# One attention tile further ahead, the hidden-layer halves moved to the end of each step, and a wider PSUM ring for the last products

## The chip, the cores and the metric

One core of a Trainium2 chip runs the whole program. The metric is the device time of one execution in microseconds; below, a number without a unit is in microseconds. TensorE is called PE, VectorE DVE, ScalarE ACT, GpSimd POOL, and SyncE, which issues the transfers, SP.

## The reference

Three layers follow each other on 1536 tokens (2 batches of 768) of width 512.

```python
# attention: 8 heads of 64; local window |i-j| < 16, plus 24 block summaries
k_sum = k.reshape(B, H, nb, 32, D).max(axis=3);  v_sum = v.reshape(...).mean(axis=3)
scores = concat(mask_local(scale * q @ k.T), scale * q @ k_sum.T + log(32))
a = softmax(scores);  x = a @ concat(v, v_sum)
# mixture of 8 experts, width 1024: all experts on all tokens, Sinkhorn weights P (8 rounds)
x = sum_e P[:, e] * (relu(x @ w1[e]) @ w2[e])
# last layer, width 2048, with a rational activation
h = x @ w_in;  y = (poly3(h; a) / (1 + |b0||h| + |b1|h^2 + 1e-6)) @ w_out
```

## The kernel before, in words

All large products are done in three passes of a split into a high and a low part (`mm3`, lines 184 to 186), so PE carries most of the work. Nothing is reordered by a planner: every engine takes its instructions in the order in which the program writes them, and an instruction that waits holds up all that stand behind it on its engine.

**Attention** works on tiles of 64 tokens (24 of them; `QT`, `NQ`) in a loop of 27 steps `s`. A tile `t` passes through these functions:
- `scores(t)`: 16 matmuls into one PSUM tile `sc` (one buffer), then four mask-and-minimum instructions on DVE (L631) that write the SBUF tile `a` (three buffers).
- `exps(t)`: four exponentials on ACT (L641).
- `norm(t)`: three DVE instructions, add (L651), reciprocal (L652) and multiply (L653). The small results of the first two lie in spare columns of the PSUM tile `xo` for `t` below 11 and in the SBUF tile `sm` after that.
- `trans(t)`: four transposes on PE (L659) into a PSUM tile `tr` (two buffers), copied out by ACT (L661).
- `av(t)`: 16 matmuls (L678) into the PSUM tile `xo`, then the split of the result into `xh` (ACT, L687) and `xl` (DVE, L688).

Step `s` writes, for PE, `scores(s)`, `av(s-3)`, half of its share of the first expert's work, `trans(s-2)`, in steps 3 to 5 three filler matmuls (`spin(3)`), the transposes of coming k or q tiles (`prep_k`, `prep_q`), and the other half of its share. For DVE it writes the masks of `scores(s)`, the `xl` of `av(s-3)`, the post of a hidden tile if one is due (`hl`, L263), and `norm(s-1)`. The share is one or two half products a step from step 7 on (`share`, `main`); a half of the first product (`g1_halves`) has six matmuls of 256 columns, a half of the second (`g2_halves`) six of 512.

The start is special. Tiles 0 to 2 are scored while data still arrives. Step 2 sums the first two blocks of v (`prep_v`). Step 3 does `trans(1)`, `exps(3)`, `norm(2)`, the last block of v, a copy of v's block means on DVE into the value tile `vx[0]` (L568), q's second tile (`prep_q(0, 1)`) and `av(0)`. POOL then copies the means into `vx[1]` and `vx[2]` (`block_values`) at the end of that step. POOL also makes the block keys and the edges of the key windows ready (`blocks_to`, `halos`). At step 15, `gate_parts` (lines 356 to 359) prepares the expert gate with one ACT and three DVE instructions.

**The experts** run afterwards in 60 blocks `block(v, j)`, each with seven products of 384 columns (L1229 to L1231) and, in `g2w`, six groups of six matmuls of 512 columns into PSUM tiles `p_v`, each added to the result by one DVE instruction (L1341). These tiles come from a ring of three (`psm`); from the third half unit on (`v >= VG`) the six groups of a block stand together. In block (1, 1) DVE does the first part of a conversion of the last layer's weights (`cv_join(0)`) ahead of `product(5)`'s hidden tile.

Of the kernel before, what the change touches and what calls it, by code (L numbers as in the profile page):

```python
# [10 lines left out]
F32 = mybir.dt.float32  # L11
# [11 lines left out]
def kernel(  # L23
# [330 lines left out]

    def gate_parts():
        nc.scalar.activation(coef[:, 4:6], coef[:, 4:6], AF.Abs)
        nc.vector.tensor_scalar_mul(coef[:, 0:4], coef[:, 0:4], -1.0)
        nc.vector.tensor_copy(wgs[:, :, 0:NE], wgr)
        nc.vector.tensor_sub(wgs[:, :, 32:32 + NE], wgr, wgs[:, :, 0:NE].bitcast(F32))


    TPIECE = HT // 4
# [3 lines left out]
    with ExitStack() as actx:  # L366
# [163 lines left out]
        def prep_q(b, i):  # L530
            new_q(b, i)
            for par in range(2):
                place(qT[b, i], par, transpose8("q", b, i, par), qscale, (b, i) == (0, 2))
# [13 lines left out]
            nc.gpsimd.tensor_add(s, t[:, :, 0, :], t[:, :, 1, :])  # L547
            nat["vsum", b, i] = s

        def prep_v(b, *parts):  # L550
            if parts[0] == 0:
                vps[b] = psm.tile([P, DM], F32, tag="mm", name=f"vps_{b}")
            ps = vps[b]
            nb = LT // BLK
            for i in parts:
                o = (NB - nb) - nb * i
                if i == NL - 1:
                    t = nat.pop(("v", b, i))
                    rs_ = [t[:, :, y, :] for y in range(2)]
                else:  # L560
                    rs_ = [nat.pop(("vsum", b, i))]
                for n, r in enumerate(rs_):
                    nc.tensor.matmul(
                        ps[SO:SO + NB, :].rearrange("p (h d) -> p h d", h=H), lhsT=wavg[:, o:o + NB], rhs=r,
                        start=(i == 0), stop=n == 1, tile_position=(0, SO),
                    )
            if parts[-1] == NL - 1:
                nc.vector.tensor_copy(vx[0][SO:SO + NB, :], ps[SO:SO + NB, :])  # L568
                vs[b] = vx[0]

        def means_split(i):
            x = nat.pop(("vsum", 1, i)).rearrange("p h d -> p (h d)")
# [32 lines left out]
        def scores(t):  # L605
            b, r = divmod(t, QB)
            qt = qT[b, r // TPL]
            if t == 1:
                ps = [psa.tile([P, NP, P], F32, tag="tr", name=f"sc_{t}_{x}", bufs=2) for x in range(2)]
            else:  # L610
                ps = psa.tile([P, 2, NP, P], F32, tag="sc", name=f"sc_{t}")
                ps = [ps[:, x] for x in range(2)]
            w = kw[:, slot(t)]
            i = 0 if r == 0 else (2 if r == QB - 1 else 1)
            m = masks[i]
            o = r % TPL * QT
            for p in range(NP):
                x = p % 2
                p = x * (NP // 2) + p // 2
                for j in range(2):  # L620
                    h = slice(j * D, (j + 1) * D)
                    y = (j ^ x) * D
                    nc.tensor.matmul(
                        ps[x][y:y + D, p % (NP // 2), 0:CO], lhsT=qt[h, p, o:o + QT], rhs=w[h, p, :],
                        start=True, stop=True, tile_position=(j * D, y),
                    )
            a = apool.tile([P, NP, CO], F32, tag="a", name=f"a_{t}", bufs=3)
            sm = apool.tile([P, 4, NP], F32, tag="sm", name=f"sm_{t}", bufs=3)
            for p in range(NP):
                p = p % 2 * (NP // 2) + p // 2  # L630
                nc.vector.tensor_tensor_reduce(  # L631
                    out=a[:, p, :], in0=ps[p // (NP // 2)][:, p % (NP // 2), 0:CO], in1=m[:, 0, :],
                    scale=-1.0, scalar=3.0e38, op0=ALU.add, op1=ALU.min, accum_out=sm[:, 0, p:p + 1],
                )
            st[t] = (a, sm, a)

        def exps(t):
            a, sm, x = st[t]
            for p in range(NP):
                p = p % 2 * (NP // 2) + p // 2  # L640
                nc.scalar.activation(  # L641
                    a[:, p, :], x[:, p, :], AF.Exp, scale=-1.0, bias=sm[:, 0, p:p + 1], accum_out=sm[:, 1, p:p + 1]
                )

        def norm(t):
            a, sm, _ = st[t]
            e, r = sm[:, 2, :], sm[:, 3, :]
            if t < QB - 1:
                o = st["xo"]
                e, r = o[:, 0, QT:QT + NP], o[:, 1, QT:QT + NP]  # L650
            nc.vector.tensor_scalar_add(e, sm[:, 1, :], 1e-9)  # L651
            nc.vector.reciprocal(r, e)  # L652
            nc.vector.tensor_mul(a, a, r.unsqueeze(2).to_broadcast([P, NP, CO]))  # L653

        def trans(t):
            a = st.pop(t)[0]
            ps = psa.tile([P, NP * P], F32, tag="tr", name=f"at_{t}", bufs=2)
            for p in range(NP):
                nc.tensor.transpose(ps[0:CO, p * P:(p + 1) * P], a[:, p, :], ident)  # L659
            aT = apool.tile([CO, NP * P], F32, tag="aT", name=f"aT_{t}")  # L660
            nc.scalar.copy(aT, ps[0:CO, :])  # L661
            st[t, "aT"] = aT
# [121 lines left out]
        def at(s, f, *args):  # L784
            todo.setdefault(s, []).append(lambda: f(*args))
# [8 lines left out]
        for i in range(NL):  # L794
            if i:
                at(8 + i, edge_after, 1, i)
            at(8 + i, halos, 1, i)
        at(10, blocks_to, 1, 0, TPL)
        at(12, blocks_to, 1, TPL, QB)
        at(3, load_nat, k, "k", 1, 0)  # L800
# [6 lines left out]
        at(15, load_tok, q, "q", 1, 2)  # L807
        at(7, load_nat, v, "v", 1, 0)
        at(8, load_nat, v, "v", 1, 1)
        at(8, load_tok, q, "q", 1, 0)  # L810
        at(9, load_nat, v, "v", 1, 2, 8)
        at(5, dma_w, 0, 2, 0, 6)
        at(7, dma_w, 0, 2, 1)
        for t in range(1, 3):
            at(3, block_values, t)
        order = [(7 + i, "k", 1, i) for i in range(NL)]
# [6 lines left out]
            at(W1[c][1], low_w1, c)  # L823
            at(W2[c], split_w2, c)
        for i in range(NL):
            at(min(8 + i, 9), block_keys, 1, i)
            at(9 + i, sum_v, 1, i)
        for i in range(NL):
            at(10 + i, means_split, i)
# [25 lines left out]
                    mains.append((ready, 0, f, NCH, h))  # L855
        share = dict(zip(range(7, 26), (2, 2, 2, 2, 2, 2, 2, 2, 2, 2, 1, 1, 2, 2, 2, 1, 1, 2, 2)))

        def main(s, end):
            n = share.get(s, 0)
            for _ in range((n + 1) // 2 if end and n < 3 else n // 2 if not end and n < 3 else 1 if end else 2):  # L860
                assert mains[0][0] <= s
                mains.pop(0)[2]()

        for s in range(NQ + AV):
            if s == 2:
                norm(0)
            if s < NQ:
                scores(s)
            if s == 2:
                prep_v(0, 0)  # L870
                prep_v(0, 1)
                norm(1)
                exps(2)
                trans(0)
                by_token_half(0)
                by_token_half(1)
            if s == AV:
                trans(1)
                exps(3)
                norm(2)  # L880
                prep_v(0, 2)
                prep_q(0, 1)
            if s >= AV:
                av(s - AV)
                if s - AV + 3 < NQ:
                    load_vx(s - AV + 3)
                flush()
            main(s, False)
            if AV < s < NQ + AV - 1:
                trans(s - AV + 1)  # L890
            if 2 < s < 6:
                spin(3)
            if AV < s <= NQ:
                norm(s - 1)
            if s < NQ and s not in (2, AV):
                exps(s)
            for f in todo.pop(s, []):
                f()
            main(s, True)
        assert not todo  # L900
        flush()
        assert not mains[0][4]
# [301 lines left out]

    late = []
    held = []

    def step(v):
        tick()

    def block(v, j):
# [9 lines left out]
        def tt(i):  # L1221
            return lambda t: (th[i][:, t, ot:ot + n], tl[i][:, t, ot:ot + n])
# [83 lines left out]
        nc.vector.tensor_add(s3, s3, Y)  # L1306
        hidden(1, 1, s3)
        step(v)
        if first:
            cv_join(0)  # L1310
        product(5, X, tt(2), False)
        hidden(1, 0, X)
        step(v)
        product(6, Y, xs(1, o2), False)
        nc.vector.tensor_add(s2, s2, Y)
# [7 lines left out]
    def g2w(v, j, half, t):  # L1323
        g = (j * HT + half * NW) // P + t
        u = UW + v // 2
        ps = psm.tile([P, 512], F32, tag="mm", name=f"p2_v{v}_{g}")
        o = t * P

        def get(c):
            hh, hl = ht["v", v, j, c, half]  # L1330
            return (hh[:, o:o + P], hl[:, o:o + P]), wt["v", v, c]

        mm3(ps, 2, get)
        a, e = acc[g], u // UPE
        if e == 0:
            nc.vector.tensor_add(a, a, ps)
        else:
            if u == UPE and v % 2 == 0:
                assert not jobs
                acc_scale(g)  # L1340
            nc.vector.scalar_tensor_tensor(  # L1341
                out=a, in0=ps, scalar=Pt[:, g, e:e + 1], in1=a, op0=ALU.mult, op1=ALU.add
            )
        if v == NSUB - 1:
            jobs.append((point[0] + 2, lambda: to_x(g)))
# [107 lines left out]
```

## Time and profile before

| | us |
|---|---|
| median of 3 runs (1358.25 to 1358.62) | 1358.3 |
| the profiled execution | 1359.21 |
| its span, from the first to the last instruction | 1357.5 |

| engine | busy in the span | share |
|---|---|---|
| PE | 1346.4 | 99% |
| DVE | 1056.3 | 78% |
| POOL | 805.3 | 59% |
| ACT | 511.9 | 38% |

Busy time of PE runs to the modelled end of each matmul, and the next one may begin before that end. So a short wait of PE does not show as idle time; it shows as a longer distance between the starts of two matmuls. The attention loop lasts from about 13 to 106 of the span, the expert blocks with the wide ring's candidates (`v >= VG`) from about 206 to 1068.

### The profile page before, as it was taken

Reading aid. Unit: us, or ns where it says so; the run is one execution under the profiler, and the core shown is the slowest. Engines: PE = TensorE matmul, PEld = TensorE weight load, DVE = VectorE, ACT = ScalarE, POOL = GpSimd, SP = SyncE. Lnnn points to the kernel's source line nnn. Section 1 sums busy time; section 2 is a strip of 40 time slices with the busy share of each in tenths; the row PEclk is TensorE's granted clock in tenths of the full one; section 3 lists DMA queues with packets and bytes.
Section 4 is the critical chain, followed back from the end, with each engine's and each line's share of the span. In section 5 each row is a group of like instructions: output and inputs, shape, how many; then the busy total and the mean of one; then the engine's idle time right before and its main releaser. Section 6 shows DMA issues by size and latency. Waiting matters only on the chain.

```text
span 1357.5 us, 20289 instructions
## 1 busy us (share of the span) xinstructions
PE 1346.4 (99%) x7343; PEld 1183.8 (87%) x7343; DVE 1056.3 (78%) x1959; ACT 511.9 (38%) x1134; POOL 805.3 (59%) x982
## 2 busy tenths in 40 slices
PE   8999999999999999999999999999999999999999
PEld 6878998889988899988999988999888888888887
DVE  7875588777777777777777777777777689988885
ACT  6874323322222222222222222222222369866662
POOL 7714647777776777777777776777777013222221
PEclk9999999999999999999999999999999999999999
DMA  9730112222222222222222222222222421213102
GB/s 260 168 84 1 47 35 74 76 83 71 78 68 72 67 68 76 68 80 72 85 75 74 67 72 69 68 76 67 83 70 65 134 74 47 89 37 93 31 16 78
DMA packets 122004, 102.40 MB, mean 75 GB/s; under 512 B 36272, under 2 KB 102960, under 8 KB 121904
## 3 DMA queue, kind: packets, MB, share of 16 engines
q1 hardware_dynamic: 121904, 101.10, 25.8%
q8 instruction: 58, 0.95, 0.3%
q14 instruction: 42, 0.34, 0.1%
HBM read 81.15 MB, written 19.92 MB: 74 GB/s over the span
## 4 chain that ended last, share of the span: by engine, by line
PE 96%; DVE 2%; ACT 1%; DMA 1%; issue 0%; SPq 0%; POOL 0%; DVEq 0%; ACTq 0%
PE p_v L184 12%; PE p_v L185 12%; PE p_v L186 12%; PE p L184 8%; PE p L186 8%; PE p L185 8%; PE X L1229 6%; PE X L1231 6%; PE X L1230 6%; PE Z L1231 3%; PE Z L1230 3%; PE Z L1229 3%; PE Y L1231 2%; PE Y L1230 2%; PE Y L1229 2%; PE xo L678 1%
## 5 line engine op out<-in xcount | busy, mean ns | idle before, releaser
L1341 DVE SCALAR_TENSOR_TENSOR accs<-p_v,Pt,accs 128x512 f32<-128x512 f32 x336 | 244.3, 745 | 89.5 <-PE p_v L186 88.8
L184 PE MATMUL p_v<-w2h_v,hh_v 128*128 128x512 f32 x720 | 283.3, 393 | 0.2
L186 PE MATMUL p_v<-w2h_v,hl_v 128*128 128x512 f32 x720 | 281.7, 391 | 0.0
L185 PE MATMUL p_v<-w2l_v,hh_v 128*128 128x512 f32 x720 | 281.5, 391 | 0.0
L1238 DVE SCALAR_TENSOR_TENSOR hl_v<-s,hh_v 128x384 fp32r<-128x384 f32 x180 | 137.5, 764 | 75.8 <-ACT hh_v L1237 74.6
L234 POOL TENSOR_TENSOR hl<-ta,hh 128x512 fp32r<-128x512 f32 x48 | 62.4, 1301 | 204.6 <-ACT hh L233 152.9
L1249 ACT COPY s<-X 128x384 f32<-128x384 f32 x56 | 27.1, 483 | 410.4 <-PE X L1231 410.4
L1039 POOL TENSOR_SCALAR ce<-ce 128x296 uint32<-128x296 uint32 (+1 forms) x56 | 67.2, 1200 | 180.2 <-DVE ce L1030 180.2
L184 PEld LDWEIGHTS p_v<-w2h_v,hh_v 128*128 128x128 f32 x720 | 135.2, 188 | 31.8 <-issue 6.2
L186 PEld LDWEIGHTS p_v<-w2h_v,hl_v 128*128 128x128 f32 x720 | 135.1, 188 | 28.7
L185 PEld LDWEIGHTS p_v<-w2l_v,hh_v 128*128 128x128 f32 x720 | 135.2, 188 | 25.5
L1237 ACT ACTIVATE hh_v<-s 128x384 fp32r<-128x384 f32 x180 | 94.9, 527 | 126.7 <-DVE s L1272 68.8
L110 POOL TENSOR_TENSOR wS<-S,wS 128x256 fp32r<-128x256 f32 x120 | 100.0, 834 | 14.4 <-ACT wS L107 4.7
L184 PE MATMUL p<-xh,w1h 128*128 128x512 f32 (+2 forms) x272 | 101.3, 373 | 0.0
L186 PE MATMUL p<-xh,w1l 128*128 128x512 f32 (+2 forms) x272 | 99.0, 364 | 0.0
L185 PE MATMUL p<-xl,w1h 128*128 128x512 f32 (+2 forms) x272 | 98.9, 364 | 0.0
L184 PE MATMUL p<-w2h,hh 128*128 128x512 f32 (+1 forms) x240 | 94.2, 392 | 0.0
L186 PE MATMUL p<-w2h,hl 128*128 128x512 f32 (+1 forms) x240 | 93.2, 389 | 0.0
L185 PE MATMUL p<-w2l,hh 128*128 128x512 f32 (+1 forms) x240 | 93.1, 388 | 0.0
L110 POOL TENSOR_TENSOR w2l_v<-sb,w2h_v 128x512 fp32r<-128x512 f32 x60 | 82.8, 1380 | 5.0
L1231 PE MATMUL X<-th,wS 128*128 128x384 f32 x240 | 80.2, 334 | 0.0
L1230 PE MATMUL X<-tl,wS 128*128 128x384 f32 x240 | 80.2, 334 | 0.0
(249 smaller groups left out, 3312.0 us busy)
## 6 DMA issues: line engine op xcount, KB each, us to landing
sa<-in_moe_w_dram SPq DMA_DIRECT2D x30, 512.0 KB, 3.5
sb<-in_moe_w_dram SPq DMA_DIRECT2D x30, 512.0 KB, 4.3
cv<-in_moe_w_in_dram SPq DMA_DIRECT2D x24, 296.0 KB, 2.9
w1h<-f_in SPq DMA_DIRECT2D x16, 256.0 KB, 2.9
w1l<-f_in SPq DMA_DIRECT2D x16, 256.0 KB, 3.2
w2h<-f_out SPq DMA_DIRECT2D x16, 256.0 KB, 4.3
w2l<-f_out SPq DMA_DIRECT2D x16, 256.0 KB, 4.8
vx<-in_v_dram SPq DMA_DIRECT2D x20, 192.0 KB, 4.2
```

The costliest lines, as they stand in the source:

```text
L110: nc.gpsimd.tensor_sub(lo, src, hi.bitcast(F32))
L184: nc.tensor.matmul(ps, lhsT=sh, rhs=mh, start=(i == 0), stop=False)
L185: nc.tensor.matmul(ps, lhsT=sh, rhs=ml, start=False, stop=False)
L186: nc.tensor.matmul(ps, lhsT=sl, rhs=mh, start=False, stop=(i == n_k - 1))
L234: nc.gpsimd.tensor_sub(hl[:, :n], ta, hh[:, :n].bitcast(F32))
L1039: nc.gpsimd.tensor_scalar(out=e, in0=e, scalar1=896, scalar2=0, op0=ALU.subtract, op1=ALU.max)
L1229: nc.tensor.matmul(ps, lhsT=w[:, 0, t], rhs=mh, start=start and t == 0, stop=False, **go)
L1230: nc.tensor.matmul(ps, lhsT=w[:, 0, t], rhs=ml, start=False, stop=False, **go)
L1231: nc.tensor.matmul(ps, lhsT=w[:, 1, t], rhs=mh, start=False, stop=t == 1, **go)
L1237: nc.scalar.activation(hh, src, AF.Relu)
L1238: nc.vector.scalar_tensor_tensor(out=hl, in0=src, scalar=0.0, in1=hh.bitcast(F32), op0=ALU.max, op1=ALU.subtract)
L1341: nc.vector.scalar_tensor_tensor(out=a, in0=ps, scalar=Pt[:, g, e:e + 1], in1=a, op0=ALU.mult, op1=ALU.add)
```

## The change

- `scores` and `exps` of step `s` are those of tile `s+1` from step 4 on (tile 4 is scored at the end of step 3).
- `trans(s-2)` becomes the first PE work of a step from step 5 on, ahead of `scores(s+1)`; `av(s-3)` follows; all half products of a step come at its end.
- Step 3 has no `av`; step 4 has `av(0)` and `av(1)`. Step 3 puts `prep_q(0, 1)` ahead of v's last block, which is split into two calls with `scores(4)` between them, and ends with `trans(2)`. Only steps 4 and 5 have filler matmuls.
- `norm` always keeps its small results in the PSUM tile `xo`.
- `block_keys(1, 2)` moves from step 9 to 10; q's tile 3 is loaded at the end of step 7 instead of in step 8, into a part of `accs` instead of a buffer of the ring `nat`.
- `gate_parts` uses ACT for two and POOL for one of its three DVE instructions.
- In block (1, 1) `cv_join(0)` stands behind the hidden tile of `product(5)`.
- For `v >= VG`, two of five `p_v` tiles come from a second PSUM pool with two buffers (`psb`).

```diff
@@ -356,5 +356,5 @@
         nc.scalar.activation(coef[:, 4:6], coef[:, 4:6], AF.Abs)
-        nc.vector.tensor_scalar_mul(coef[:, 0:4], coef[:, 0:4], -1.0)
-        nc.vector.tensor_copy(wgs[:, :, 0:NE], wgr)
-        nc.vector.tensor_sub(wgs[:, :, 32:32 + NE], wgr, wgs[:, :, 0:NE].bitcast(F32))
+        nc.scalar.mul(coef[:, 0:4], coef[:, 0:4], -1.0)
+        nc.scalar.copy(wgs[:, :, 0:NE], wgr)
+        nc.gpsimd.tensor_sub(wgs[:, :, 32:32 + NE], wgr, wgs[:, :, 0:NE].bitcast(F32))
 
@@ -549,22 +549,21 @@
 
-        def prep_v(b, *parts):
-            if parts[0] == 0:
-                vps[b] = psm.tile([P, DM], F32, tag="mm", name=f"vps_{b}")
-            ps = vps[b]
+        def mean_rows(ps, i, r, **flags):
             nb = LT // BLK
-            for i in parts:
-                o = (NB - nb) - nb * i
-                if i == NL - 1:
-                    t = nat.pop(("v", b, i))
-                    rs_ = [t[:, :, y, :] for y in range(2)]
-                else:
-                    rs_ = [nat.pop(("vsum", b, i))]
-                for n, r in enumerate(rs_):
-                    nc.tensor.matmul(
-                        ps[SO:SO + NB, :].rearrange("p (h d) -> p h d", h=H), lhsT=wavg[:, o:o + NB], rhs=r,
-                        start=(i == 0), stop=n == 1, tile_position=(0, SO),
-                    )
-            if parts[-1] == NL - 1:
+            o = (NB - nb) - nb * i
+            nc.tensor.matmul(
+                ps[SO:SO + NB, :].rearrange("p (h d) -> p h d", h=H), lhsT=wavg[:, o:o + NB], rhs=r,
+                tile_position=(0, SO), **flags,
+            )
+
+        def prep_v(b, i):
+            if i == 0:
+                vps[b] = psm.tile([P, DM], F32, tag="mm", name=f"vps_{b}")
+            mean_rows(vps[b], i, nat.pop(("vsum", b, i)), start=i == 0, stop=False)
+
+        def prep_v_end(y):
+            ps = vps[0]
+            mean_rows(ps, NL - 1, nat["v", 0, NL - 1][:, :, y, :], start=False, stop=y == 1)
+            if y:
                 nc.vector.tensor_copy(vx[0][SO:SO + NB, :], ps[SO:SO + NB, :])
-                vs[b] = vx[0]
+                vs[0] = vx[0]
 
@@ -646,6 +645,4 @@
             a, sm, _ = st[t]
-            e, r = sm[:, 2, :], sm[:, 3, :]
-            if t < QB - 1:
-                o = st["xo"]
-                e, r = o[:, 0, QT:QT + NP], o[:, 1, QT:QT + NP]
+            o = st["xo"]
+            e, r = o[:, 0, QT:QT + NP], o[:, 1, QT:QT + NP]
             nc.vector.tensor_scalar_add(e, sm[:, 1, :], 1e-9)
@@ -797,2 +794,4 @@
             at(8 + i, halos, 1, i)
+        for i in range(NL):
+            at(8 + i, block_keys, 1, i)
         at(10, blocks_to, 1, 0, TPL)
@@ -809,3 +808,2 @@
         at(8, load_nat, v, "v", 1, 1)
-        at(8, load_tok, q, "q", 1, 0)
         at(9, load_nat, v, "v", 1, 2, 8)
@@ -813,2 +811,3 @@
         at(7, dma_w, 0, 2, 1)
+        at(7, load_tok, q, "q", 1, 0, 0)
         for t in range(1, 3):
@@ -825,3 +824,2 @@
         for i in range(NL):
-            at(min(8 + i, 9), block_keys, 1, i)
             at(9 + i, sum_v, 1, i)
@@ -857,8 +855,2 @@
 
-        def main(s, end):
-            n = share.get(s, 0)
-            for _ in range((n + 1) // 2 if end and n < 3 else n // 2 if not end and n < 3 else 1 if end else 2):
-                assert mains[0][0] <= s
-                mains.pop(0)[2]()
-
         for s in range(NQ + AV):
@@ -866,5 +858,10 @@
                 norm(0)
-            if s < NQ:
-                scores(s)
-            if s == 2:
+            if AV + 1 < s < NQ + AV - 1:
+                trans(s - AV + 1)
+            t = s if s <= AV else s + 1
+            if t < NQ:
+                scores(t)
+            if s < 2:
+                exps(s)
+            elif s == 2:
                 prep_v(0, 0)
@@ -876,25 +873,29 @@
                 by_token_half(1)
-            if s == AV:
+            elif s == AV:
                 trans(1)
+                prep_q(0, 1)
                 exps(3)
+                prep_v_end(0)
                 norm(2)
-                prep_v(0, 2)
-                prep_q(0, 1)
-            if s >= AV:
-                av(s - AV)
-                if s - AV + 3 < NQ:
-                    load_vx(s - AV + 3)
+                scores(4)
+                prep_v_end(1)
+                exps(4)
+                trans(2)
+            else:
+                for i in range(s - AV if s > AV + 1 else 0, s - AV + 1):
+                    av(i)
+                    if i + 3 < NQ:
+                        load_vx(i + 3)
                 flush()
-            main(s, False)
-            if AV < s < NQ + AV - 1:
-                trans(s - AV + 1)
-            if 2 < s < 6:
-                spin(3)
-            if AV < s <= NQ:
-                norm(s - 1)
-            if s < NQ and s not in (2, AV):
-                exps(s)
+                if s < 6:
+                    spin(3)
+                if s <= NQ:
+                    norm(s - 1)
+                if t < NQ:
+                    exps(t)
             for f in todo.pop(s, []):
                 f()
-            main(s, True)
+            for _ in range(share.get(s, 0)):
+                assert mains[0][0] <= s
+                mains.pop(0)[2]()
         assert not todo
@@ -1206,2 +1207,3 @@
     held = []
+    ring = [0]
 
@@ -1308,6 +1310,6 @@
         step(v)
-        if first:
-            cv_join(0)
         product(5, X, tt(2), False)
         hidden(1, 0, X)
+        if first:
+            cv_join(0)
         step(v)
@@ -1325,3 +1327,6 @@
         u = UW + v // 2
-        ps = psm.tile([P, 512], F32, tag="mm", name=f"p2_v{v}_{g}")
+        if v >= VG:
+            ring[0] += 1
+        pool, tag = (psb, "g") if ring[0] % 5 > 2 else (psm, "mm")
+        ps = pool.tile([P, 512], F32, tag=tag, name=f"p2_v{v}_{g}")
         o = t * P
```

## Rows read from the trace of the kernel before

**Rows 1.** The page, busy time of PE

```profile
PE 1346.4 (99%) x7343; PEld 1183.8 (87%) x7343; DVE 1056.3 (78%) x1959; ACT 511.9 (38%) x1134; POOL 805.3 (59%) x982
```

**Rows 2.** Stretch: busy per engine, granted clock, DMA share, GB/s

```profile
8.00:12.00 4.00, 2.53 (x20) 1.89 (x19) 3.64 (x5) 1.77 (x3) 2.48 (x6) 1.00 1.20 288
```

**Rows 3.** Timeline, step 18: start, duration, engine, operation [idle before <-releaser]

```profile
78.14 0.64 PE L623 MATMUL sc<-kw,qs 64*64 64x120 f32 x16
...
78.71 0.69 PE L678 MATMUL xo<-aT,vx 120*64 120x64 f32 x16
...
79.44 0.37 ACT L687 CAST xh<-xo 128x256 fp32r<-128x256 f32 x1 [0.43 <-PE xo L678]
...
79.85 0.42 DVE L688 TENSOR_TENSOR xl<-xo,xh 128x256 fp32r<-128x256 f32 x1
...
80.19 0.16 DVE L651 TENSOR_SCALAR sm<-sm 128x4 f32<-128x4 f32 x1
...
80.59 0.66 DVE L653 TENSOR_TENSOR a<-a,sm 128x480 f32<-128x480 f32 x1
```

**Rows 4.** Timeline of step 17, DVE, where a hidden tile's post is due

```profile
77.17 0.41 DVE L263 SCALAR_TENSOR_TENSOR hl<-p,hh 128x256 fp32r<-128x256 f32 x1
...
77.50 0.16 DVE L651 TENSOR_SCALAR sm<-sm 128x4 f32<-128x4 f32 x1
```

**Rows 5.** Timeline of step 5, DVE, small results in PSUM

```profile
27.91 0.42 DVE L688 TENSOR_TENSOR xl<-xo,xh 128x256 fp32r<-128x256 f32 x1 [0.27 <-ACT xh L687]
...
28.37 0.17 DVE L651 TENSOR_SCALAR xo<-sm 128x4 f32<-128x4 f32 x1
```

**Rows 6.** Timeline of PE from step 5 to step 6

```profile
26.02 0.64 PE L623 MATMUL sc<-kw,qs 64*64 64x120 f32 x16
...
27.21 0.65 PE L659 MATMUL at<-ident,a 128*120 128x128 f32 x4
...
27.70 0.83 PE L540 MATMUL spin<-ident 128*128 128x128 f32 x6
...
28.46 0.64 PE L623 MATMUL sc<-kw,qs 64*64 64x120 f32 x16
```

**Rows 7.** Timeline of PE, the scores of steps 15 and 16

```profile
66.55 0.64 PE L623 MATMUL sc<-kw,qs 64*64 64x120 f32 x16
...
69.80 0.64 PE L623 MATMUL sc<-kw,qs 64*64 64x120 f32 x16
```

**Rows 8.** Timeline of PE, its waits in steps 10 and 17

```profile
47.33 0.63 PE L427 MATMUL qps<-ident,q 128*128 128x128 f32 x4 [0.72 <-DVE sm L631]
...
74.61 0.64 PE L623 MATMUL sc<-kw,qs 64*64 64x120 f32 x16 [1.50 <-DVE sm L631]
...
76.16 0.65 PE L659 MATMUL at<-ident,a 128*120 128x128 f32 x4 [0.30 <-DVE a L653]
```

**Rows 9.** Timeline of the expert blocks, PE and DVE

```profile
206.46 0.41 PE L1229 MATMUL X<-xh,wA 128*128 128x384 f32 x1 [0.32 <-DVE hl_v L1238]
...
252.46 2.05 DVE L1341 SCALAR_TENSOR_TENSOR accs<-p_v,Pt,accs 128x512 f32<-128x512 f32 x3
...
252.90 0.39 PE L186 MATMUL p_v<-w2h_v,hl_v 128*128 128x512 f32 x1
253.34 0.47 PE L184 MATMUL p_v<-w2h_v,hh_v 128*128 128x512 f32 x1
...
1032.10 0.47 PE L184 MATMUL p_v<-w2h_v,hh_v 128*128 128x512 f32 x1
```

**Rows 10.** Timeline of copies in step 3, block keys and scores later

```profile
19.04 0.62 ACT L521 COPY accs<-q 128x512 f32<-128x512 f32 x1
...
22.44 1.32 POOL L388 TENSOR_SCALAR vx<-vx 24x512 f32<-24x512 f32 x2 [4.96 <-DVE vx L568]
...
50.15 0.51 POOL L388 TENSOR_SCALAR kw<-ks 128x384 f32<-128x384 f32 x1
...
53.20 0.64 PE L623 MATMUL sc<-kw,qs 64*64 64x120 f32 x16
```

More of the change, by code (lines that the diff above doesn't have):

```diff
@@ L548, in sum_v @@
             nat["vsum", b, i] = s
-        def prep_v(b, *parts):
-            if parts[0] == 0:
-                vps[b] = psm.tile([P, DM], F32, tag="mm", name=f"vps_{b}")
-            ps = vps[b]
-            nb = LT // BLK
-            for i in parts:
-                o = (NB - nb) - nb * i
-                if i == NL - 1:
-                    t = nat.pop(("v", b, i))
-                    rs_ = [t[:, :, y, :] for y in range(2)]
-                else:
-                    rs_ = [nat.pop(("vsum", b, i))]
-                for n, r in enumerate(rs_):
-                    nc.tensor.matmul(
-                        ps[SO:SO + NB, :].rearrange("p (h d) -> p h d", h=H), lhsT=wavg[:, o:o + NB], rhs=r,
-                        start=(i == 0), stop=n == 1, tile_position=(0, SO),
-                    )
-            if parts[-1] == NL - 1:
+        def mean_rows(ps, i, r, **flags):
+            nb = LT // BLK
+            o = (NB - nb) - nb * i
[5 more added lines that the diff above has]
+            if i == 0:
+                vps[b] = psm.tile([P, DM], F32, tag="mm", name=f"vps_{b}")
+            mean_rows(vps[b], i, nat.pop(("vsum", b, i)), start=i == 0, stop=False)
[3 more added lines that the diff above has]
+            if y:
                 nc.vector.tensor_copy(vx[0][SO:SO + NB, :], ps[SO:SO + NB, :])
-                vs[b] = vx[0]
+                vs[0] = vx[0]
         def means_split(i):
@@ L1308, in block @@
         step(v)
+        product(5, X, tt(2), False)
+        hidden(1, 0, X)
         if first:
             cv_join(0)
-        product(5, X, tt(2), False)
-        hidden(1, 0, X)
         step(v)
```

## Prediction

> **What bounds the kernel now.** I read the page's busy times first: PE 1346.4 of a span of 1357.5 [rows 1]. The reader is to see two things in that: only 11 of idle time are left to be won in the open, and whatever delays PE is paid in full. Then I went through the timeline of the attention loop, where the change works, and wrote down for each step which engine's instruction let PE go on. There PE is fed by a chain through ACT and DVE, and the time of a step is the larger of PE's work and that chain. Before the change PE's work is the larger nearly everywhere. Last I looked at the expert blocks by the distances between matmul starts, because a short wait does not show as idle time there.
>
> **The chain of one step.** Step 18 shows it with little in its way [rows 3]: the scores start 0.57 ahead of `av` (78.14, 78.71); `xh` starts 0.73 after `av`, `xl` 0.41 after `xh`, the norm's first instruction 0.34 after `xl`, and the norm ends at 80.59 + 0.66 = 81.25. So from the start of `av` to the end of the norm it is 2.54. Two additions: with the norm's small results in PSUM the norm starts 0.46 after `xl` instead of 0.34 [rows 5], which now holds for all tiles; where a hidden tile's post stands between, `xl`, post and norm take 0.34 + 0.33 = 0.67 [rows 3, 4].
>
> In the old order `norm(s-1)` has until the middle of the next step before `trans(s-1)` asks for it: the scores, `av` and half a share of PE work lie between. In the new order `trans` stands first on PE, and `scores`, `av` and everything else stand behind it in PE's queue. Who waits for them in turn is the next norm, because its place on DVE is behind the masks of `scores(s+1)` and the `xl` of `av(s-3)` of the same step. That closes a ring: `trans`, scores, `av`, `xh`, `xl`, norm, next `trans`. Its length: trans 0.49 [rows 6], scores 0.57, then 2.54 + 0.12 to the norm's end, and some 0.1 to PE (my estimate; PE waits for just this in step 17 [rows 8]): 3.8. With a post it is 0.33 - 0.12 longer, the transposes a little shorter behind fp32r matmuls: 4.0. A step cannot be shorter than that, whatever PE has to do. Scoring one tile further ahead does not open the ring, as the norm is of tile s-1 and its exponentials were done two steps before.
>
> **The start (to the first half products).** A step of PE work is 28.46 - 26.02 = 2.44, with filler [rows 6]. The transposes of tiles 3, 4 and 5 each come at the ring's pace: 3 x (3.8 - 2.44) = 4.1 of waiting. `scores(8)` now follows its q tile's copies directly; both are on ACT behind `exps(7)`: 0.7. q's second tile now stands ahead of v's last block, but its copies end at 19.04 + 0.62 = 19.66 [rows 10]; PE, done with `trans(1)` at about 19.2 (18.7 and 0.49), waits 0.5, and v's block no longer fills that. `av(1)` follows `av(0)` at once and needs the means that POOL copies; POOL took up the old pair 0.5 after DVE and needs 0.66 for each [rows 10]: about 0.4 of waiting. Off go one filler, 28.46 - 27.70 = 0.76 [rows 6], and two old waits of together 0.4. Sum: 4.1 + 0.7 + 0.5 + 0.4 - 0.8 - 0.4 = +4.5. Bounds: +1 if only the single waits stay, +6 if each of the three steps also pays for ACT.
>
> **The middle (steps 8 to 13).** These steps carry k or q tiles or 512-column halves, 4.1 to 4.6 of PE work (by the distances of the scores' starts, of which that before 53.20 [rows 10] is the widest), so the ring costs nothing but 0.3 in each of two steps where the block maxima stand before the masks on DVE. `scores(12)` comes a step sooner. Its block keys end on POOL at 50.66 against scores at 53.20 [rows 10]: 2.5 of slack, less than the 4.6 of the step that is skipped, and POOL's queue runs some later than before since `block_values` started later. I take 1.75, bounds 0 and 2.5. The wait of 0.72 in step 10 [rows 8] goes: DVE, which the row names, had no work for that tile, so I put it down to the second of q's transfers, which the change issues a step earlier on SP, ahead of v's second block; if that is wrong the 0.7 stays. Joining the two half products saves one change between fp32 and fp32r matmuls per step, about 0.1 (estimate), over eight steps 1.0 with the prepared tiles. Sum: 0.6 + 1.75 - 0.7 - 1.0 = +0.6.
>
> **The second half (steps 14 to 26).** A step with two 256-column halves and no prepared tile took 69.80 - 66.55 = 3.25 [rows 7], 3.15 with the halves joined; its ring is 4.0: 0.85 of waiting. A step with one half has 2.4 of work: 1.55. By the share there are four of the first kind whose wait shows in full, one whose post goes through ACT alone (0.6), one at 0.85 from a 512-column half, and two of the second kind (1.55 and 1.3). With 0.4 of single waits they make 8.0. Off go the wait of 1.50 in step 17 and that of 0.30 behind it [rows 8]: they come from DVE instructions of `gate_parts`, now on ACT and POOL, and from norms slowed while POOL works, which the PSUM place avoids. On POOL the subtraction stands ahead of sums that the logits stage needs 30 later, so nothing waits for it. With 0.3 of smaller waits and 1.2 from joined halves: 8.0 - 2.1 - 1.2 = +4.7, less 0.2 by which my old starts stand late here: +4.5. Bounds: -3 (no ring at all) and +7.
>
> **The expert blocks.** In every second block the fourth group of `p_v` starts 0.44 behind its predecessor instead of 0.23 [rows 9]: it needs the first group's PSUM tile, which DVE frees at 252.46 + a third of 2.05 = 253.14, late because it was still busy with hidden tiles. Twenty blocks from this one to the one at 1032.10 [rows 9] show it, by 0.05 to 0.33; summed over the lengths of all blocks against the shortest, it is 3.7. With five tiles the fourth group asks for one of the block before: all 3.7 go (bounds 0 and 3.7). Behind block (1, 1) PE waits 0.32 in the open [rows 9], 0.5 by the distance of starts, for the hidden tile that `cv_join(0)` delays; that goes too. Sum: -4.2.
>
> **Total.** 4.5 + 0.6 + 4.5 - 4.2 = +5.4; I take off 0.2 for the old waits that my chain makes a little too long. The span goes from 1357.5 to 1362.7, the profiled execution from 1359.2 to 1364.4. That execution was 0.9 above the median of the runs, so the median goes from 1358.3 to 1363.5.
>
> **A rule on the clock.** PE waited a third of the time between 8 and 12 (2.53 busy of 4.00) and kept its full granted clock, 1.00, which is 2.4 GHz [rows 2]; the new start has the same share. The Trainium skill ("TensorE: Matmul & The Clock Gate", section "What's actually happening") says that the gate follows how busy PE has lately been and falls to half rate when it is not; one filler fewer and 1.3 of waiting per step point that way. By the row the sum stays; by the rule it would be the fourth rival's.
>
> **Rivals.**
> - *The ring is open.* The norm is ready in time in all steps, so that scoring ahead does what it says. For it: DVE is busy only 78% [rows 1]. Against it: order, not load, makes the ring. Then the waits of steps 10 and 17, the filler, the changes of type and the experts' 4.2 are all won: 0.7 + 1.8 + 0.8 + 1.5 + 4.2 = 9.0, 1349.3, faster. It decides if `trans` starts less than 0.2 after the PE instruction before it from step 5 on. Chance 0.10.
> - *The ring binds only at the start*, since a step's later halves cover it. The second half is then -2.8: 4.5 + 0.6 - 2.8 - 4.2 = -1.9, 1356.4. Against it: 3.15 is less than 4.0. Chance 0.13.
> - *The wider PSUM ring gives nothing*, because DVE is late as a whole and the wait moves to the next group: 1363.5 + 4 = 1367.5. Against it: DVE idles inside the blocks. Chance 0.08.
> - *The clock falls* to 1.2 GHz between 25 and 40: the 2.44 of a step doubles and passes the ring's 3.8 by 1.1, in four steps +4: 1367.7. Chance 0.07.
>
> **How the numbers follow.** The forecast has 0.62. Its own range is 1360 to 1367. A change of less than 0.2% (2.7) cannot be told from none. Slower: nearly all of the forecast and the last two rivals, 0.73. Same: most of the second rival and the forecast's lower tail, 0.15. Faster: the first rival and a little of the second, 0.12. The range leaves out the first rival and some of either end: 1357.0 to 1367.8.
>
> **What would show it.** The timeline after should have `trans(3)`, `trans(4)`, `trans(5)` on PE with idle time of over 1 each, released by L653; steps 5 to 7 some 3.8 apart; steps with two short halves 4.0 apart instead of 3.25; `scores(12)` waiting for POOL; no wait at the logits' gate step; and no distance of 0.44 in `p_v`. The prediction is wrong if PE does not wait for L653 in steps 16 to 25, or if the attention loop ends less than 5 later than before.

## The result, and the profile after

The changed kernel takes 1366.36 (median of six runs, 1366.02 to 1367.46); beside it the kernel before took 1358.61 (six runs, 1358.25 to 1360.49). The ratio is 1.0056, with an interval of 1.0043 to 1.0069: slower by 7.75. The forecast was 1363.5, the range 1357.0 to 1367.8, and slower had a chance of 0.73. Direction and mechanism came out as said; in the sum one term, the saving from joined halves, was not there. Of the six runs two, the slowest (1367.36 and 1367.46), had a mean granted clock of 0.999 where the others had 1.000.

The profiled execution after took 1366.04, with a span of 1364.3, so the spans differ by 6.8. The rest of the 7.75 is where the profiled executions lie: that of before 0.6 above its median, that of after 0.3 below.

The busy times first (engine, busy time, share of the span, instructions), from the page of the kernel after:

```profile
PE 1344.2 (99%) x7337; PEld 1185.2 (87%) x7337; DVE 1050.2 (77%) x1956; ACT 512.1 (38%) x1136; POOL 803.9 (59%) x983
```

PE does 2.2 less than before [rows 1] in a span that is 6.8 longer: what was added is waiting. The waits of PE between 12 and 125 say on whom (what waits, the releaser, then total, number and longest):

```profile
PE at L656 <- DVE a L650: 10.1, 11, 1.6
PE sc L622 <- POOL kw L388: 1.5, 1, 1.5
...
PE sc L622 <- ACT qs L440: 0.2, 1, 0.2
PE xo L675 <- POOL vx L388: 0.2, 1, 0.2
```

Eleven times the transposes, now first in a step, wait for the norm's multiply (L650 here, L653 before). The second line is `scores(12)` waiting for its block keys, 1.5 where I had 1.75. The last two are single waits of the start, `scores(8)` for its q tile and `av(1)` for v's means, 0.2 each where I had 0.7 and 0.4.

The timeline of PE at the start of the loop (start, duration, line, output from inputs; in brackets the idle time before and its releaser):

```profile
25.30 0.94 PE L540 MATMUL spin<-ident 128*128 128x128 f32 x6
27.84 0.62 PE L656 MATMUL at<-ident,a 128*120 128x128 f32 x4 [1.60 <-DVE a L650]
...
29.58 0.94 PE L540 MATMUL spin<-ident 128*128 128x128 f32 x6
31.70 0.65 PE L656 MATMUL at<-ident,a 128*120 128x128 f32 x4 [1.18 <-DVE a L650]
...
35.67 0.62 PE L656 MATMUL at<-ident,a 128*120 128x128 f32 x4 [1.11 <-DVE a L650]
```

`trans(3)`, `trans(4)` and `trans(5)` each wait over 1, and the steps are 3.86 and 3.97 apart, against 2.44 in the old order [rows 6]. The same ring a good 50 later (lines of PE, ACT and DVE picked out of one timeline). The step from 76.22 has two short halves, that from 80.28 one half of 512 columns:

```profile
76.22 0.62 PE L656 MATMUL at<-ident,a 128*120 128x128 f32 x4 [0.71 <-DVE a L650]
...
80.28 0.65 PE L656 MATMUL at<-ident,a 128*120 128x128 f32 x4 [0.62 <-DVE a L650]
80.86 0.64 PE L622 MATMUL sc<-kw,qs 64*64 64x120 f32 x16
81.43 0.69 PE L675 MATMUL xo<-aT,vx 120*64 120x64 f32 x16
...
82.16 0.37 ACT L684 CAST xh<-xo 128x256 fp32r<-128x256 f32 x1 [0.56 <-PE xo L675]
...
82.57 0.42 DVE L685 TENSOR_TENSOR xl<-xo,xh 128x256 fp32r<-128x256 f32 x1
...
82.91 0.41 DVE L263 SCALAR_TENSOR_TENSOR hl<-p,hh 128x256 fp32r<-128x256 f32 x1
...
83.24 0.15 DVE L648 TENSOR_SCALAR xo<-sm 128x4 f32<-128x4 f32 x1
...
83.65 0.65 DVE L650 TENSOR_TENSOR a<-a,xo 128x480 f32<-128x480 f32 x1
...
84.36 0.65 PE L656 MATMUL at<-ident,a 128*120 128x128 f32 x4 [0.66 <-DVE a L650]
```

From 80.28 on each line waits for the one above it or stands behind it on its engine, round to the next transposes: 84.36 - 80.28 = 4.08 for the ring, and 4.06 for the step before. PE's own work is 3.25 in a step with two short halves [rows 7], and 3.24 in this one, as experiment 1 shows.

In the expert blocks the fourth group of `p_v` no longer stands 0.44 behind its predecessor [rows 9]; between 222 and 1073 no distance is over 0.26. The end of the third group and the start of the fourth in the block of [rows 9], after:

```profile
263.62 0.39 PE L186 MATMUL p_v<-w2h_v,hl_v 128*128 128x512 f32 x1
263.85 0.39 PE L184 MATMUL p_v<-w2h_v,hh_v 128*128 128x512 f32 x1
```

### The profile page after: what moved, and what is told of

It reads as the page before. It is cut to its first block, busy times and chain, and to the rows that moved or that the text cites. A ratio compares the mean times of both kernels' runs of the same rounds, so it can differ in the third digit from the quotient of the medians.

```text
span 1364.3 us, 20260 instructions
## 1 busy us (share of the span) xinstructions
PE 1344.2 (99%) x7337; PEld 1185.2 (87%) x7337; DVE 1050.2 (77%) x1956; ACT 512.1 (38%) x1136; POOL 803.9 (59%) x983
## 4 chain that ended last, share of the span: by engine, by line
PE 94%; DVE 2%; ACT 2%; DMA 1%; issue 0%; POOL 0%; SPq 0%; ACTq 0%; DVEq 0%
PE p_v L185 12%; PE p_v L184 12%; PE p_v L186 12%; PE p L184 8%; PE p L186 8%; PE p L185 8%; PE X L1233 6%; PE X L1231 6%; PE X L1232 6%; PE Z L1233 3%; PE Z L1232 3%; PE Z L1231 3%; PE Y L1233 2%; PE Y L1232 2%; PE Y L1231 2%; PE xo L675 1%
```

## The experiments

The ratios are to the kernel before, run on the same chip.

**1. The norm ahead of the scores' masks.** This opens the ring: in the kernel after, the norm of tile s-1 no longer stands behind the masks and the `xl` of its step.

```diff
             # right behind trans, ahead of scores
+            if AV < s <= NQ:
+                norm(s - 1)
...
-                if s <= NQ:
-                    norm(s - 1)
```

> The changed kernel with norm(s-1) put ahead of the masks of scores(s+1) on DVE, right behind trans(s-2); nothing else moves. Theory A (the ring trans, scores, av, xh, xl, norm, next trans sets the length of a step): the ring is cut, the 10.1 us in which PE waits for L650 in the attention loop all but go, and the time falls by about 9 us, from 1366.4 to some 1357.5 (1355.5 to 1360). Theory B (the loss comes from the order of PE's work itself, trans ahead of scores and all half products at the end): the order on PE is unchanged, so the time stays within 2 us of 1366.4.

Measured: 1360.32 (ten runs, 1359.43 to 1362.77), ratio 1.0017 (1.0007 to 1.0027). That is 0.3 above the range of theory A and far from theory B. Two of PE's waits in the same stretch, the longest and the one at the transposes:

```profile
PE sc L622 <- ACT qs L440: 2.2, 1, 2.2
...
PE at L656 <- DVE a L650: 0.4, 1, 0.4
```

The waits at the transposes go from 10.1 to 0.4 and the last `av` comes 6.4 sooner (116.00 to 109.59). Two steps, one with two short halves and one with a half of 512 columns, are now 3.25 and 3.24 long, PE's own work; in the kernel after they took 4.06 and 4.08:

```profile
74.57 0.60 PE L656 MATMUL at<-ident,a 128*120 128x128 f32 x4
...
77.82 0.60 PE L656 MATMUL at<-ident,a 128*120 128x128 f32 x4
...
81.06 0.60 PE L656 MATMUL at<-ident,a 128*120 128x128 f32 x4
```

So the norm's place on DVE carries about 6 of the 7.75: what is left is 1.9 above the kernel before (1358.38 beside these runs). Nearly all of the 6.4 is won in the second half of the loop. At `av(10)` it is only 0.7 (64.43 to 63.77). At the start the open ring uncovers other single waits; the longest is `scores(8)` waiting for its q tile's copies, 2.2 instead of 0.2. `av(4)` starts at 35.88 there, against 37.12 in the kernel after and 31.78 before, so most of the start's loss stays without the ring.

**2. The post behind the norm.** A smaller cut at the same ring: it takes the hidden tile's post (L263) out and leaves the rest.

```diff
             # after the second of the step's PE groups
-                flush()
...
                 if s <= NQ:
                     norm(s - 1)
+                flush()
```

> The changed kernel with the post of a hidden tile (relu, hl) behind the norm in each step. Theory A (ring): a step that is bound by the ring and has a hidden tile's post gets 0.33 us shorter less the 0.11 us that the norm waits for xl, so starts of trans in steps 16 to 18 are 3.85 us apart instead of 4.08; over some seven such steps the time falls by 1.5 us, to 1364.9 (1363.9 to 1365.7). Theory B (DVE as a whole is too slow in these steps): the work on DVE is the same and so is the time, 1366.4.

Measured: 1365.22 (four runs, 1364.89 to 1368.03), 1.0050 (1.0035 to 1.0065); 1.1 less than the kernel after, at the edge of what can be told. The timeline shows what the time leaves unsure:

```profile
76.52 0.62 PE L656 MATMUL at<-ident,a 128*120 128x128 f32 x4 [0.51 <-DVE a L650]
...
80.37 0.65 PE L656 MATMUL at<-ident,a 128*120 128x128 f32 x4 [0.42 <-DVE a L650]
...
84.25 0.66 PE L656 MATMUL at<-ident,a 128*120 128x128 f32 x4 [0.46 <-DVE a L650]
```

The ring is 3.85 and 3.88 instead of 4.06 and 4.08, for one post less. That is the 0.33 that the post took less the 0.12 by which the norm then waits for `xl`: a member that leaves the ring shortens the step by what it had added, so the ring sets the step.

**3. Joined halves alone.** The kernel before, with a step's half products all at its end.

```diff
-            main(s, False)
...
-            main(s, True)
+            for _ in range(share.get(s, 0)):
+                mains.pop(0)[2]()
```

> The kernel before with the joined half products alone. Theory A: 1.2 us less than before, 1357.2; trans waits for the norm at most in steps 15 to 17, where the norm is slow while POOL works. Theory B: 3 us more or above.

Measured: 1358.31 (ten runs, 1356.98 to 1359.70), 0.9997 (0.9988 to 1.0007). In time this decides nothing: the 1.2 of theory A is not there, and neither is the loss of theory B. The last `av` starts 0.8 sooner (104.34 against 105.12): less than the 2.2 that my sum has for it. Three short waits of the transposes for the norm, together 1.0 where the kernel before has 0.3, take some of it back.

**4. The same, with the transposes first.** No scoring ahead, and the old start.

```diff
             # first PE work of the step; on top of experiment 3
+            if AV < s < NQ + AV - 1:
+                trans(s - AV + 1)
...
-            if AV < s < NQ + AV - 1:
-                trans(s - AV + 1)
```

> The kernel before with the joined half products and with trans(s-2) as the first PE work of a step, ahead of scores(s) and av(s-3); nothing is scored further ahead, and the start is the old one. Theory A (the place of trans closes the ring; scoring ahead is no part of it): waits of over 1 us on L653 in steps 5 to 7 and of 0.6 us and more in steps 16 to 25, and 8 us above the joined halves alone, 1365.5 (1363 to 1368). Theory B (the loss comes from scoring a tile further ahead and from the new start): no more than 1 us above the joined halves alone.

Measured: 1371.38 (four runs, 1370.58 to 1372.09), 1.0096 (1.0081 to 1.0111). Slower than the range of theory A, and its last `av` starts at 117.75, later than that of the whole change (116.00). The waits of PE:

```profile
PE at L659 <- DVE a L653: 8.7, 8, 2.0
PE at L659 <- ACT a L641: 5.0, 6, 1.4
```

The first line is the ring again. The second names the exponentials, but it is the ring too, as one of these waits shows:

```profile
80.58 0.66 DVE L653 TENSOR_TENSOR a<-a,sm 128x480 f32<-128x480 f32 x1
...
81.06 0.19 ACT L641 ACTIVATION_READ_ACCUMULATOR a<-a,sm 128x1 f32 x1
...
81.38 0.62 PE L659 MATMUL at<-ident,a 128*120 128x128 f32 x4 [0.71 <-ACT a L641]
```

The exponentials that end at 81.25 are those of the next tile and only end last; those of the tile transposed here ended at 75.79. The norm's multiply ends at 81.24, and the transposes start 0.14 after it. The four other waits of this kind inside the loop start 0.14 or 0.15 after a multiply too, as do most of those that name L653. So the loss comes from the place of the transposes. That scoring one tile ahead helps against it is not shown: in this step the exponentials were ready 4.4 before the norm took them up at 80.17. What makes this kernel slower than the whole change is above all two norms with their factors in SBUF while POOL works (last section). They take 2.18 and 2.38 (69.45 to 71.63, 74.71 to 77.09) where that of 80.17 takes 1.07, and from `av(11)` to `av(13)` this kernel needs 10.73 (67.64, 78.37), the kernel after 8.34 (69.00, 77.34).

**5. The wide ring alone.** The kernel before with the second PSUM pool for `p_v` and `cv_join(0)` behind the hidden tile.

```diff
+        if v >= VG:
+            ring[0] += 1
+        pool, tag = (psb, "g") if ring[0] % 5 > 2 else (psm, "mm")
+        ps = pool.tile([P, 512], F32, tag=tag, name=f"p2_v{v}_{g}")
-        ps = psm.tile([P, 512], F32, tag="mm", name=f"p2_v{v}_{g}")
```

> The kernel before with the expert blocks' part of the change alone: two of five p_v tiles from the second PSUM pool and cv_join(0) behind the hidden tile of product(5). Theory A (the part is a gain of its own that the attention loop's loss hides): 3.9 us less than before, 1354.7 (the two traces have the last block 10.9 and 7.0 us apart at the ends of that stage). Theory B (the blocks only caught up since they started later): no change, 1358.6.

Measured: 1355.11 (1354.91 to 1356.58), 0.9974 (0.9965 to 0.9984): 3.3 faster than the kernel before beside it. It is a gain of its own that the loop's loss covers in the whole change. At the start of the last full block the trace has 4.1 (1043.60 to 1039.48).

**6. No filler at all.** The kernel after without the fillers of steps 4 and 5.

```diff
-                if s < 6:
-                    spin(3)
```

> The changed kernel without the two fillers of steps 4 and 5. Theory A (PE waits for the norm there in any case): the waits on L650 grow by what the fillers took, 0.8 us each, and the time stays within 0.5 us of 1366.4. Theory B (the fillers are on PE's path): 1.5 us less, 1364.9. Theory C (the clock falls when PE waits more): granted clock below 1.00 in the stretch from 25 to 40 us and a time 2 us or more above.

Measured: 1368.47 (four runs, 1366.82 to 1369.36), 1.0068 (1.0053 to 1.0083). Work was removed, and the time rose by 2.1, as theory C had it. Two stretches of the kernel after (from and to, length, busy time of PE, PEld, DVE, ACT and POOL, granted clock, DMA share, GB/s):

```profile
24.00:32.00 8.00, 5.06 (x83) 4.11 (x82) 5.35 (x26) 5.11 (x21) 7.83 (x15) 1.00 0.81 198
32.00:36.00 4.00, 2.88 (x47) 2.28 (x45) 2.72 (x13) 3.00 (x12) 4.00 (x6) 1.00 0.75 201
```

and of the kernel without fillers:

```profile
24.00:32.00 8.00, 3.50 (x84) 2.58 (x74) 4.90 (x25) 5.37 (x23) 7.40 (x14) 0.87 0.87 213
32.00:36.00 4.00, 3.84 (x40) 3.08 (x41) 1.93 (x11) 1.26 (x5) 3.11 (x4) 0.50 0.47 138
```

with PE's timeline in it:

```profile
28.27 0.62 PE L656 MATMUL at<-ident,a 128*120 128x128 f32 x4 [2.47 <-DVE a L650]
28.82 0.64 PE L622 MATMUL sc<-kw,qs 64*64 64x120 f32 x16
29.39 0.73 PE L675 MATMUL xo<-aT,vx 120*64 120x64 f32 x16
32.16 1.11 PE L656 MATMUL at<-ident,a 128*120 128x128 f32 x4 [2.04 <-DVE a L650]
```

Idle for 2.47 and, after less than 2 of work, for 2.04, PE comes out with a granted clock of 0.50, which is 1.2 GHz, and the same transposes take 1.11 instead of 0.62. The Trainium skill ("TensorE: Matmul & The Clock Gate", section "What's actually happening") says that the gate grants the rate by how busy PE has lately been; the row agrees, and the fourth rival's mechanism is real. The fillers are worth their place although nothing needs their result: with them PE idles 1.60 and 1.18 here, and the clock stays at 1.00.

**7. A longer filler.** The kernel after with `spin(6)` for `spin(3)`: are the fillers themselves on the path?

```diff
-                    spin(3)
+                    spin(6)
```

> The changed kernel with fillers of six instead of three in steps 4 and 5. Theory A (PE waits for the norm there in any case, and the filler keeps its clock): the waits on L650 in steps 5 and 6 shrink by what the fillers take more, 0.7 us each, trans starts at the same times, and all runs lie within 0.5 us of 1366.2. Theory B (fillers are on PE's path): 1.5 us more, 1367.8.

Measured: 1366.13 (four runs, 1366.06 to 1366.31), 1.0049 (1.0034 to 1.0064). PE:

```profile
25.23 1.60 PE L540 MATMUL spin<-ident 128*128 128x128 f32 x12
27.77 0.62 PE L656 MATMUL at<-ident,a 128*120 128x128 f32 x4 [0.93 <-DVE a L650]
...
31.62 0.65 PE L656 MATMUL at<-ident,a 128*120 128x128 f32 x4 [0.51 <-DVE a L650]
```

Each filler took 0.66 more, and each wait shrank by as much; the transposes start where they did. The chain through ACT and DVE sets the start, PE has room. All four runs lie within 0.25.

**8. All but the loop's order.** The kernel before with the wide ring, `cv_join(0)`, the new `gate_parts`, the earlier q load and the norm's small results in PSUM for all tiles.

```diff
-            e, r = sm[:, 2, :], sm[:, 3, :]
-            if t < QB - 1:
-                o = st["xo"]
-                e, r = o[:, 0, QT:QT + NP], o[:, 1, QT:QT + NP]
+            o = st["xo"]
+            e, r = o[:, 0, QT:QT + NP], o[:, 1, QT:QT + NP]
...
-        nc.vector.tensor_copy(wgs[:, :, 0:NE], wgr)
+        nc.scalar.copy(wgs[:, :, 0:NE], wgr)
...
-        at(8, load_tok, q, "q", 1, 0)
+        at(7, load_tok, q, "q", 1, 0, 0)
```

> The kernel before with everything of the change but the attention loop's new order: the wide ring and cv_join(0), gate_parts off DVE, the norm's small results in PSUM for all tiles, q's tile 3 loaded at the end of step 7. Theory A (the loss lies in the loop's order alone, and these parts are gains): 3.3 us for the expert blocks, 1.8 us for the waits of step 17, 0.7 us for the wait of step 10, so 1352.6 (1351.5 to 1354). Theory B (the waits of steps 10 and 17 went in the changed kernel only because the loop ran later): 1355.1, as with the wide ring alone.

Measured: 1354.94 (1354.84 to 1355.26), 0.9971 (0.9962 to 0.9981). That is outside the range of theory A: by the time alone these parts add nothing to the wide ring's 1355.11, as theory B had it, but not for its reason. `av(14)` starts at 73.61 instead of 75.18, so most of the wait of step 17 [rows 8] is gone, and it is lost again further on. PE, and the norm's multiply on DVE:

```profile
94.28 0.65 DVE L651 TENSOR_TENSOR a<-a,xo 128x480 f32<-128x480 f32 x1
...
95.04 0.69 PE L676 MATMUL xo<-aT,vx 120*64 120x64 f32 x16 [0.57 <-ACT a L641]
...
97.05 0.65 DVE L651 TENSOR_TENSOR a<-a,xo 128x480 f32<-128x480 f32 x1
...
97.81 0.69 PE L676 MATMUL xo<-aT,vx 120*64 120x64 f32 x16 [0.79 <-ACT a L641]
```

The brackets name exponentials, but both `av`s start 0.11 after the end of a norm's multiply (94.93, 97.70). The output tile `xo` of `av` is the one in which that norm keeps its small results, so `av` waits for the norm. The norm in turn stands directly behind `xl` or the post on DVE and does not wait for exponentials (93.87 and 96.63, 0.33 and 0.46 after the instruction before it). So `av`, `xh`, `xl`, norm and the next `av` make a second ring. The wait of step 10 went too, and an `av` waited 0.82 at 48.83 instead.

**9. The same with joined halves** (the diffs of 8 and 3 together).

> The same with all half products of a step joined at its end, behind trans and the prepared tiles; trans stays behind scores and av. Theory A (joining saves one change between fp32 and fp32r matmuls per step, about 0.1 us, and breaks nothing, since trans still comes 1.2 us after the start of the step): 1.2 us less than without it, 1351.4. Theory B (joining is what makes PE wait for the norm): waits on L653 as in the changed kernel and 3 us more or above.

Measured: 1353.46 (five runs, 1353.39 to 1354.65), 0.9966 (0.9953 to 0.9979): 1.5 below experiment 8. Here the joining pays: the last `av` starts 1.3 sooner (104.81 to 103.49). 1.2 of waiting for `xo` is left.

**10. PSUM for the norm only up to tile 17.** Experiment 9, with SBUF for the tiles behind, which fall where POOL is idle.

```diff
-            if t < QB - 1:
+            if t < 18:
```

> As the joined halves on top of all but the loop's order, with the norm's small results in PSUM only for tiles below 18 and in SBUF after that, when POOL is idle. Theory A (in that kernel av waits in steps 22 and 23 for the exponentials, since its PSUM tile is held by a norm that waits for them): the 1.2 us of waits in xo on L641 go, and the time is 1352.3 (1351.8 to 1353.0). Theory B (PE would wait for the same exponentials at trans a little later): 1353.5, unchanged.

Measured: 1352.25 (four runs, 1352.16 to 1352.40) against 1359.20 for the kernel before beside it, 0.9947 (0.9930 to 0.9964): faster than both kernels, by 7.0 and some 14. Of the 1.2 of waits for `xo` none is left, as theory A had it, though what held `xo` was the norm and not the exponentials (experiment 8). The two longest and the last wait for 12 to 125 are now

```profile
PE sc L623 <- POOL accs L547: 0.8, 1, 0.8
PE sc L623 <- issue: 0.4, 1, 0.4
...
PE at L659 <- DVE a L653: 0.2, 1, 0.2
```

## Why the prediction was right, and where its sum was off

The stretches are read from the starts of the same `av` in both traces, less 1.05 where the new order has done scores and transposes ahead of it.

- **The ring** was predicted as "trans, scores, `av`, `xh`, `xl`, norm, next trans" and is that, link by link. Experiments 1, 2 and 4 show it as the cause: take the norm out and the waits go; take the post out and the step shrinks by what it had added; keep only the place of the transposes and the loss stays. The first rival (the ring is open) and the second (it binds only at the start) fall: PE waits for L650 in eight steps from 76.22 on.
- **The start:** +4.5 predicted, +4.3 measured (`av(4)` 31.78 to 37.12, less 1.05). The two single waits came out 0.7 smaller together; the two distances between the three transposes, which I had at 3.8, are 3.9 and 4.0. That the ring alone costs the 4.1 of the sum is not shown: without it (experiment 1) `av(4)` starts only 1.2 sooner.
- **The middle:** +0.6 predicted, +0.7 measured, with luck. `scores(12)` and the wait of step 10 came out nearly as said (1.5, and 0.7 gone). But neither the 0.6 of the ring nor the 1.0 of joined halves shows: the five other distances from `av(4)` to `av(10)` are 4.09, 4.14, 4.19, 4.57 and 4.59, and were 4.13, 4.11, 4.12, 4.60 and 4.60. The two misses nearly cancel.
- **The second half:** +4.5 predicted, +5.9 measured (`av(23)` 105.12 to 116.00, less what stood before it). This is the stretch that was mis-sized, by 1.4, and the term in it is the 1.2 taken off for joined halves. In experiment 1, where PE does not wait, a step with joined halves and the transposes first takes 3.25 (74.57, 77.82), just what it took before [rows 7], and not 3.15. The two halves are shorter, 1.53 against 1.70, but the transposes take 0.53 to the next start (74.57, 75.10) where they took 0.36 (68.56, 68.92 in the kernel before): the new place gives back what joining saves. With the transposes in their old place joining saved 0.8 (experiment 3) and 1.3 (experiment 9) over the whole loop, where I had 2.2. The ring is longer than I had it as well, 4.06 to 4.08 and not 4.0: I took the transposes a little shorter behind fp32r matmuls, but when PE has waited they keep their full 0.58 to the scores (80.28, 80.86). So the wait of such a step, 4.07 less 3.25, is the 0.8 that the sum had. Its items add up to 8.1 and not to the 8.0 written there; the 0.2 of the miss that is left is not separated.
- **The expert blocks:** -4.2 predicted, -3.9 measured (10.9 later at the end of the loop, 7.0 at the last full block). The wider PSUM ring gave what was predicted: the block that starts its `p_v` groups at 217.99 does so at 228.71 after, 10.7 later, and from there to the last full block 3.75 is won, against 3.7. The term that fell short is the 0.5 for `cv_join(0)`. The block at 206.46 does start only 10.4 later, at 216.85, but 0.3 is lost again at once:

```profile
220.45 0.39 PE L186 MATMUL p_v<-w2h_v,hl_v 128*128 128x512 f32 x1
220.96 0.50 PE L184 MATMUL p_v<-w2h_v,hh_v 128*128 128x512 f32 x1
```

  In experiment 5 the same distance is 0.52. I put it down to `cv_join(0)`, which took 2.25 on DVE in its new place and 1.44 in the old one; no run moves it alone. The third rival, that the wider PSUM ring gives nothing, falls.
- **The clock** stayed at 1.00 in the profiled execution, as the rows of before had it and not as the fourth rival had it. Experiment 6 shows how near it was: without the last two fillers it falls.

Summed from the starts: 4.3 + 0.7 + 5.9 - 0.2 - 3.7 = 7.0, against 6.8 between the spans.

## What to carry to other kernels

Before moving an instruction to the head of an in-order queue, follow what stands behind it round to its own input: if the way back leads through other engines' queues, that way is the shortest step there can be, however idle those engines are. Doing one input further ahead helps only if that input closes the ring; here the exponentials were ready in time anyway, and the norm stayed in. A bracket in a timeline names a releaser that the profile infers, and it need not be what the start waited for: compare the ends of all instructions that it needs. And where one part of a change loses and another gains, run the gaining part alone: the experts' part was worth 3.3 and could not be seen in the whole.

## What the runs showed of the hardware

**The norm's multiply and POOL.** With the small factors in SBUF, DVE's multiply took nearly twice as long while POOL added in SBUF. Two lines of the kernel before, one of DVE and one of POOL:

```profile
66.04 1.22 DVE L653 TENSOR_TENSOR a<-a,sm 128x480 f32<-128x480 f32 x1
...
64.77 4.32 POOL L785 TENSOR_TENSOR accs<-xh,xl 128x384 f32<-128x384 f32 x4
```

and the same pair in the kernel after, with the factors in PSUM:

```profile
79.57 0.65 DVE L650 TENSOR_TENSOR a<-a,xo 128x480 f32<-128x480 f32 x1
...
77.56 3.90 POOL L782 TENSOR_TENSOR accs<-xh,xl 128x384 f32<-128x384 f32 x4
```

With POOL idle the form with SBUF takes 0.66 [rows 3]. The Trainium skill ("SBUF — State Buffer", section "Who interferes with whom") says that a DVE instruction with two inputs in SBUF contends with a GpSimd instruction that reads SBUF, as its second input comes through a read interface that the two share; the three durations agree. I had expected the gain of the PSUM place, but not its price: it holds `xo` until the norm is done, and `av` waited 0.57 and 0.79 for that in experiment 8. PSUM where POOL works and SBUF where it is idle has neither (experiment 10).

**The clock fell after short waits.** After two waits of 2.47 and 2.04 with work between them the clock was 0.50 over 32 to 36; after waits of 1.60 and 1.18 at the same places it was 1.00. A single wait of 2.16 in that stretch (experiment 1), with PE busy for 7.20 of the 8 ahead (24 to 32), left it at 1.00. I had not expected that a filler without any use to the result, hidden in a wait, would be worth 2.1.
